# Reading the moving operand of a feed-forward kernel as two interleaved streams

## The chip, the cores and the metric

The kernel runs on one core of one Trainium2 chip. TensorE does the matrix products (its weight loads are shown as an engine of their own, PEld), VectorE (DVE), ScalarE (ACT) and GpSimd (POOL) do the rest, and SyncE (SP) issues nearly all DMAs. The metric is the device time of one execution, in microseconds; lower is better.

## The reference

A dynamic convolution over the last 7 tokens, with softmaxed weights for each token and head, is followed by a feed-forward network with a squared ReLU:

```python
# x: (8, 4096, 192), weight_gen: (8, 4096, 8, 7), w_in: (192, 2048), w_out: (2048, 192), all float32
w = exp(weight_gen - max); w = w / (sum(w) + 1e-9)
out[b, s, h] = sum over k of w[b, s, h, k] * x_padded[b, s + k, h]     # 6 zero tokens ahead of each sequence
h = out.reshape(32768, 192) @ w_in
g = relu(h) ** 2
result = g @ w_out                                                      # (32768, 192)
```

## The kernel before

**Tiling.** The 32768 tokens lie on the 128 partitions, 256 consecutive tokens (`R`) on each. A chunk is 4 such rows (`TC`) of all partitions, 512 tokens (`N`), and there are 64 chunks. For each chunk the convolution runs on VectorE with tokens on partitions. The result is then turned, so that the 192 features lie on the partitions (3 blocks of 64, `D1`, each held twice, in the lower and in the upper 64 partitions) and the 512 tokens along the free dimension. VectorE turns blocks of 32x32 (`Q` is 32) and DMAs through DRAM put the blocks in place.

**Precision.** Products are made of pairs of numbers rounded to the fast float32 format: each operand has a high and a low part (`xh`, `xl`, `gh`, `gl`; `W` and `V` hold high and low parts of the weights). ScalarE makes the high part, VectorE the low part by subtraction.

**First product, `mm1(c, j)`, matmul at L430.** Two blocks of 128 hidden features at a time: 9 terms for each, each with 64 contraction rows and 512 moving columns. The two blocks' matmuls are issued in turn, one on the lower and one on the upper 64 rows of the array, so they run side by side as a pair: 9 pairs, 18 matmuls a call. The moving operand is `xx[rows, k]`, 512 consecutive float32 of a partition.

**Activation.** `relu` (L445 to L447), `square` (L451) and `high` (L455) run on ScalarE, `low` (L459) on VectorE.

**Second product, `mm2_turned(c, fb)`, matmul at L503.** The hidden features are contracted: for each block `fb` of 128 hidden features 5 pairs of matmuls with 64 rows and 512 moving columns, the moving operand being `g[rows]`, again 512 consecutive values. Chunks 1 to 62 go this way. Chunk 0 and the last chunk use `mm2_tile` instead (L467, L476), where the activations are the stationary operand and the moving operand is a slice of `V` or of decoded weights.

**Order.** The order is written out by hand. A chunk is 8 steps `j`. In each step TensorE does `mm1(c, j)` (9 pairs) and then `mm2_turned` for the two blocks of two steps earlier (10 pairs; `LAG` is 2, the wait list is `pend`). The low parts of a step are issued on VectorE in the step after it (`late`). `sum_turned` empties the accumulators at the end of a chunk's second product. In steps 5 and 6 of the next chunk `store_turned` turns the result back in blocks of 32x32 (L522, L525), 24 small DMAs (L531) put the blocks into `o_sb` with tokens on partitions again, and one DMA (L536) writes the chunk's 4 rows of every partition to `out`. `store` (L557) does that for chunk 0 and, in three pieces, for the last chunk. All these DMAs are issued from SP's queue, as are the loads (L107, L108), the move in `sum_turned` (L514) and the turn of the convolution (L399, L404).

Of the kernel before, what the change touches and what calls it, by code (L numbers as in the profile page):

```python
# [21 lines left out]
def kernel(  # L22
# [9 lines left out]
    nc = tc.nc  # L32
# [4 lines left out]
    P = 128  # L37
    Q = 32
    HALO = K - 1
    R = B * S // P  # L40
    PPB = S // R
    TC = 4
# [26 lines left out]

    x_v = x.rearrange("b s d -> (b s) d").rearrange("(p r) d -> p r d", r=R)  # L70
    wg_v = wg.rearrange("b s h k -> (b s) (h k)").rearrange("(p r) e -> p r e", r=R)
    out_v = out.rearrange("(p r) d -> p r d", r=R)
    w_in_u = w_in.bitcast(U32)
    w_out_u = w_out.bitcast(U32).rearrange("(f p) e -> p f e", p=P)

# [8 lines left out]
    def rows_of(c):  # L84
        return (c + CPG if c < CPG else c - CPG if c < 2 * CPG else c) * TC
# [323 lines left out]
    phs, rgs, ghs, gls, accs = {}, {}, {}, {}, {}  # L409

    def mm1(c, j, ops=range(9)):
        xh, xl = xts[c]["h"], xts[c]["l"]
        if (c, 2 * j) not in phs:
            if c == 0 and j < 2:
                two = [ps_o.tile([P, N], F32, name=f"acc{b + 2 - 2 * j}") for b in range(2)]
            elif c == 0 and j % 2:
                two = [ps_o.tile([P, N], F32, name=f"acc{b}") for b in (2, 3)]
            else:
                two = [ps_h.tile([P, N], F32, name="ph") for _ in range(2)]
            phs[c, 2 * j], phs[c, 2 * j + 1] = two  # L420
        two = phs[c, 2 * j], phs[c, 2 * j + 1]
        seq = [(q, xx, k) for q, xx in ((0, xh), (0, xl), (1, xh)) for k in range(ND)]
        for n, (q, xx, k) in enumerate(seq):
            if n not in ops:
                continue
            for i in range(2):
                rows = slice(i * D1, (i + 1) * D1)
                kw = (k + i) % ND if c < N_PE else k
                w = W[rows, q, j, kw * P:(kw + 1) * P]
                nc.tensor.matmul(two[i], w, xx[rows, k], start=(n == 0), stop=(n == len(seq) - 1))  # L430

    def relu(c, fb):
        ph = phs.pop((c, fb))
# [55 lines left out]
    def mm2_turned(c, fb):  # L489
        if fb == 0:  # L490
            accs[c] = [ps_o.tile([P, N], F32, name=f"acc{t}") for t in range(4)]
        gh, gl = ghs.pop((c, fb)), gls.pop((c, fb))
        j, i = divmod(fb, 2)
        first, last = fb == 0, fb == NF - 1
        A, B = [(0, 0, gh), (0, 0, gl), (0, 1, gh)], [(2, None, gh), (2, None, gl)]
        seq = B + A if last or first else A + B
        for n, (b, q, g) in enumerate(seq):
            k = sum(1 for m in seq[:n] if m[0] == b)
            for h in range(2):
                rows = slice(h * D1, (h + 1) * D1)  # L500
                w = V[rows, fb, P:2 * P] if q is None else V[rows, fb, 2 * P * q:2 * P * q + P]
                fl = dict(start=first and k == 0, stop=last and k == (2 if b == 0 else 1))
                nc.tensor.matmul(accs[c][b + h], w, g[rows], **fl)  # L503

    works = {}

# [9 lines left out]
    def store_turned(c, part):  # L516
        X = works[c]
        if part == 0:
            o_sb = op.tile([P, TC, D], F32, name="o_sb", bufs=2)
            Y = stage.tile([P, 2, N], F32, name="raw")  # L520
            outs[c] = o_sb, Y
            nc.vector.transpose(Y[:, 0], X[:, 0])  # L522
        else:
            nc.vector.tensor_tensor(out=X[0:D1, 1], in0=X[0:D1, 1], in1=X[0:D1, 2], op=ALU.add)
            nc.vector.transpose(outs[c][1][0:D1, 1], X[0:D1, 1])  # L525
        o_sb, Y = outs[c]
        y = Y[:, part].rearrange("p (t q i) -> p q t i" if c < N_PE else "p (q t i) -> p q t i", t=TC, i=Q)
        for e in range(P // Q if part == 0 else D1 // Q):
            d0 = part * P + e * Q
            for q in range(P // Q):  # L530
                nc.sync.dma_start(  # L531
                    out=o_sb[q * Q:(q + 1) * Q, :, d0:d0 + Q],
                    in_=y[e * Q:(e + 1) * Q, q],
                )
        if part:
            nc.sync.dma_start(out=out_v[:, rows_of(c):rows_of(c) + TC, :], in_=o_sb)  # L536

    outs = {}

# [12 lines left out]
                nc.vector.tensor_tensor(out=to[:, h], in0=acc[:, h], in1=tmp[:, t, l], op=ALU.add)  # L552

    def store(c, t0, t1):
        o_sb, _ = outs[c]
        tsl = slice(t0, t1)
        nc.sync.dma_start(out=out_v[:, rows_of(c) + t0:rows_of(c) + t1, :], in_=o_sb[:, tsl])  # L557


    nc.vector.memset(warm, 0.0)  # L560
# [33 lines left out]
    for u in range(NU):  # L594
# [36 lines left out]
        if u == 0:  # L631
            for n in range(2 * ND):
                for j in range(2):
                    mm1(0, j, (n,))
            for j in range(2):
                mm1(0, j, range(2 * ND, 3 * ND))
        else:
            mm1(0, 2 * u)
            mm1(0, 2 * u + 1)
# [68 lines left out]
    for c in range(1, NCH):  # L708
        tail = c == NCH - 1
        for j in range(NJ):  # L710
# [4 lines left out]
            if c == 1 and j == 0:  # L715
                for t in range(TC // 2):
                    finish(0, t)
                store(0, 0, TC)
# [3 lines left out]
            if len(pend) == LAG or tail and pend:  # L722
                c2, j2 = pend.pop(0)
                for fb in (2 * j2, 2 * j2 + 1):
                    mm2_turned(c2, fb)
                done = c2 if j2 == NJ - 1 else None
# [15 lines left out]
            if c > 1 and j == OUT_STEP:  # L742
                store_turned(c - 1, 0)
            if c > 1 and j == OUT_STEP + 1:
                store_turned(c - 1, 1)
# [4 lines left out]
    c = NCH - 1  # L750
# [7 lines left out]
    for t in range(TC - 1):  # L758
        for fb in range(NF - 4, NF):
            mm2_tile(c, fb, t)  # L760
        finish(c, t)
        if t:
            store(c, 0 if t == 1 else t, t + 1)
    t, end = TC - 1, range(NF - 4, NF)
# [6 lines left out]
    o_sb, tmp = outs[c]  # L771
    finish(c, t, tmp[:, t, 0:D])
    nc.vector.tensor_tensor(out=o_sb[:, t], in0=rest[:, 0:D], in1=tmp[:, t, 0:D], op=ALU.add)  # L773
    store(c, t, TC)


# [28 lines left out]
```

## Time and profile before

| | |
|---|---|
| time, median of 3 runs | 2230.92 us (2230.7 to 2230.98) |
| span of the profiled execution, first to last instruction | 2229.4 us |
| TensorE busy | 2224.8 us, 19486 matmuls |
| VectorE busy | 1869.8 us |
| ScalarE busy | 1805.4 us |
| GpSimd busy | 9.9 us |
| DMA | 195.30 MB, mean 88 GB/s |

The profiled execution's own time is its span and what lies around it; the median of the runs is 1.5 us above the span. The busy time of TensorE counts overlapping matmuls once. A matmul's start is recorded; its end is modelled, so the distance between starts is the figure to read, not the duration of one.

### The profile page before, as it was taken

Reading aid. Unit: us, or ns where it says so; the run is one execution under the profiler, and the core shown is the slowest. Engines: PE = TensorE matmul, PEld = TensorE weight load, DVE = VectorE, ACT = ScalarE, POOL = GpSimd, SP = SyncE. Lnnn points to the kernel's source line nnn. Section 1 sums busy time; section 2 is a strip of 40 time slices with the busy share of each in tenths; the row PEclk is TensorE's granted clock in tenths of the full one; section 3 lists DMA queues with packets and bytes.
Section 4 is the critical chain, followed back from the end, with each engine's and each line's share of the span. In section 5 each row is a group of like instructions: output and inputs, shape, how many; then the busy total and the mean of one; then the engine's idle time right before and its main releaser. Section 6 shows DMA issues by size and latency. Waiting matters only on the chain.

```text
span 2229.4 us, 50051 instructions
## 1 busy us (share of the span) xinstructions
PE 2224.8 (100%) x19486; PEld 1846.2 (83%) x19486; DVE 1869.8 (84%) x2866; ACT 1805.4 (81%) x3492; POOL 9.9 (0%) x18
## 2 busy tenths in 40 slices
PE   9999999999999999999999999999999999999999
PEld 8888888888888888888888888888888888888888
DVE  9888888888888888888898888888888888888885
ACT  8888888888888888888888888888888888888886
POOL 0000000000000000000000000000000000000000
PEclk9999999999999999999999999999999999999999
DMA  8433323333233333333332333323333233332322
GB/s 221 96 85 92 90 59 100 83 94 99 57 92 89 88 100 75 74 95 82 100 85 64 100 85 92 88 60 100 84 94 96 54 98 86 91 100 66 82 60 53
DMA packets 323117, 195.30 MB, mean 88 GB/s; under 512 B 223944, under 2 KB 281288, under 8 KB 319040
## 3 DMA queue, kind: packets, MB, share of 16 engines
q1 hardware_dynamic: 321584, 188.58, 33.8%
q0 software_dynamic: 1296, 3.54, 0.9%
q8 instruction: 152, 2.49, 0.5%
q14 instruction: 85, 0.70, 0.1%
HBM read 106.39 MB, written 49.55 MB: 70 GB/s over the span
## 4 chain that ended last, share of the span: by engine, by line
PE 100%; POOL 0%; DVE 0%; issue 0%; POOLq 0%
PE acc L503 50%; PE ph L430 46%; PE acc L467 1%; PE acc L476 1%; PE acc L430 0%; PE acc L341 0%; PE acc L567 0%; PE ph L329 0%; PE ph L770 0%; PE acc L329 0%; PE acc L767 0%; DVE o_sb L773 0%; POOL ident masks.py:199 0%; POOL ident masks.py:197 0%; POOL ex L92 0%
## 5 line engine op out<-in xcount | busy, mean ns | idle before, releaser
L503 PE MATMUL acc<-gh,V 64*128 64x512 f32 x5952 | 1007.4, 386 | 0.0
L430 PE MATMUL ph<-xh,W 64*128 64x512 f32 x6084 | 853.9, 386 | 0.0
L447 ACT ACTIVATE rg<-ph 128x512 f32<-128x512 f32 x992 | 539.1, 597 | 351.5 <-PE ph L430 351.4
L503 PE MATMUL acc<-gl,V 64*128 64x512 f32 x3968 | 772.4, 386 | 0.0
L459 DVE TENSOR_TENSOR gl<-rg,gh 128x512 fp32r<-128x512 f32 x1008 | 644.4, 678 | 139.0 <-ACT gh L455 137.4
L430 PEld LDWEIGHTS ph<-xh,W 64*128 64x128 f32 x6084 | 569.6, 184 | 120.4 <-ACT rg L445 0.4
L503 PEld LDWEIGHTS acc<-gh,V 64*128 64x128 f32 x5952 | 557.5, 184 | 117.1
L451 ACT ACTIVATE rg<-rg 128x512 f32<-128x512 f32 x1008 | 581.3, 633 | 0.2
L455 ACT CAST gh<-rg 128x512 fp32r<-128x512 f32 x1008 | 576.1, 626 | 3.2 <-PE acc L476 3.2
L503 PEld LDWEIGHTS acc<-gl,V 64*128 64x128 f32 x3968 | 371.7, 184 | 78.0
L430 PE MATMUL ph<-xl,W 64*128 64x512 f32 x3042 | 427.3, 386 | 0.0
L266 DVE TENSOR_TENSOR pr<-xt,wt 128x768 f32<-128x768 f32 (+1 forms) x441 | 411.7, 946 | 2.3
L279 DVE TENSOR_TENSOR pr<-pr 128x768 f32<-128x768 f32 x366 | 347.0, 948 | 0.1
L430 PEld LDWEIGHTS ph<-xl,W 64*128 64x128 f32 x3042 | 284.9, 184 | 59.9
L310 DVE TENSOR_TENSOR xl<-xT,xh 128x512 fp32r<-128x512 f32 x186 | 117.7, 688 | 180.9 <-ACT xh L307 180.9
L307 ACT CAST xh<-xT 128x512 fp32r<-128x512 f32 x186 | 102.7, 624 | 0.1
L513 DVE TENSOR_TENSOR raw<-acc,raw 128x512 f32<-128x512 f32 x124 | 79.9, 686 | 5.9 <-ACT raw L511 5.9
L511 ACT COPY raw<-acc 128x512 f32<-128x512 f32 x124 | 66.6, 597 | 0.0
L237 ACT ACTIVATE wt<-wt 128x224 f32<-128x224 f32 x62 | 24.3, 392 | 47.4 <-DVE wt L236 47.4
L393 DVE STREAM_TRANSPOSE xr<-pr 128x768 f32<-128x768 f32 x62 | 60.6, 978 | 2.1
L525 DVE STREAM_TRANSPOSE raw<-raw 64x512 f32<-64x512 f32 x62 | 43.6, 704 | 2.1
L522 DVE STREAM_TRANSPOSE raw<-raw 128x512 f32<-128x512 f32 x62 | 43.7, 704 | 0.0
(93 smaller groups left out, 449.8 us busy)
## 6 DMA issues: line engine op xcount, KB each, us to landing
xT<-xd SPq DMA_DIRECT2D x124, 384.0 KB, 5.0
xt<-in_x_dram SPq DMA_DIRECT2D x30, 1344.0 KB, 6.9
out_dram<-o_sb SPq DMA_DIRECT2D x63, 384.0 KB, 2.7
xd<-xr SPq DMA_DIRECT2D x248, 96.0 KB, 2.0
o_sb<-raw SPq DMA_DIRECT2D x1488, 16.0 KB, 1.8
raw<-raw SPq DMA_DIRECT2D x62, 128.0 KB, 4.2
wt<-in_weight_gen_dram SPq DMA_DIRECT2D x31, 224.0 KB, 3.2
raw<-in_moe_w_in_dram SPq DMA_DIRECT2D x16, 192.0 KB, 5.3
```

What stands on the lines that cost most here:

```text
L266: tt(out=dst, in0=src, in1=wf[:, t0 * H:t1 * H, k:k + 1].broadcast_to([P, m, G]), op=ALU.mult)
L279: tt(out=prs[k0], in0=prs[k0], in1=prs.pop(k), op=ALU.add)
L307: nc.scalar.copy(parts["h"][:, k, n], src[k][:, n])
L310: tt(out=parts["l"][:, k, n], in0=src[k][:, n], in1=parts["h"][:, k, n].bitcast(F32), op=ALU.subtract)
L430: nc.tensor.matmul(two[i], w, xx[rows, k], start=(n == 0), stop=(n == len(seq) - 1))
L447: nc.scalar.activation(r, ph, AF.Relu)
L451: nc.scalar.activation(r, r, AF.Square)
L455: nc.scalar.copy(gh, rgs[c, fb])
L459: nc.vector.tensor_tensor(out=gl, in0=rgs.pop((c, fb)), in1=ghs[c, fb].bitcast(F32), op=ALU.subtract)
L503: nc.tensor.matmul(accs[c][b + h], w, g[rows], **fl)
L511: nc.scalar.copy(X[:, k], acc[b])
L513: nc.vector.tensor_tensor(out=X[:, k], in0=acc[b + 1], in1=X[:, k], op=ALU.add)
```

## The change

Before, both products read 512 moving columns in the order in which they lie. After it, each block of 32 columns is read as columns 0, 16, 1, 17, 2, 18 and so on, two streams 16 columns (64 bytes) apart, taken in turn. The number of columns, matmuls and weight loads stays. The output columns come out in that permuted order, so the tokens of each block of 32 are permuted once (chunk 0 and the last, where only the first product reads this way) or twice (all others). The store undoes that: instead of one DMA of 128 partitions there are four, one for each group of 32 partitions, whose DRAM side walks the partitions in the turned order (`a` is 4 for two reads and 2 for one).

```diff
-    out_v = out.rearrange("(p r) d -> p r d", r=R)
+
+    def put_out(c, t0, t1, o_sb, reads):
+        rows = slice(rows_of(c) + t0, rows_of(c) + t1)
+        v = out.rearrange("(q a b r) d -> q b a r d", q=P // Q, a=2 ** reads, r=R)
+        for q in range(P // Q):
+            nc.sync.dma_start(out=v[q, :, :, rows, :], in_=o_sb[q * Q:(q + 1) * Q, t0:t1])
+
+    def two_streams(t):
+        return t.rearrange("p (b i m) -> p b m i", i=2, m=Q // 2)
...
-                nc.tensor.matmul(two[i], w, xx[rows, k], start=(n == 0), stop=(n == len(seq) - 1))
+                nc.tensor.matmul(two[i], w, two_streams(xx[rows, k]), start=(n == 0), stop=(n == len(seq) - 1))
...
-                nc.tensor.matmul(accs[c][b + h], w, g[rows], **fl)
+                nc.tensor.matmul(accs[c][b + h], w, two_streams(g[rows]), **fl)
...
         if part:
-            nc.sync.dma_start(out=out_v[:, rows_of(c):rows_of(c) + TC, :], in_=o_sb)
+            put_out(c, 0, TC, o_sb, 2)
...
     def store(c, t0, t1):
-        o_sb, _ = outs[c]
-        tsl = slice(t0, t1)
-        nc.sync.dma_start(out=out_v[:, rows_of(c) + t0:rows_of(c) + t1, :], in_=o_sb[:, tsl])
+        put_out(c, t0, t1, outs[c][0], 1)
```

## Rows read from the trace of the kernel before

**Rows 1.** The page: busy time by engine, and the chain that ended last by line.

```profile
PE 2224.8 (100%) x19486; PEld 1846.2 (83%) x19486; DVE 1869.8 (84%) x2866; ACT 1805.4 (81%) x3492; POOL 9.9 (0%) x18
...
PE acc L503 50%; PE ph L430 46%; PE acc L467 1%; PE acc L476 1%; PE acc L430 0%; PE acc L341 0%; PE acc L567 0%; PE ph L329 0%; PE ph L770 0%; PE acc L329 0%; PE acc L767 0%; DVE o_sb L773 0%; POOL ident masks.py:199 0%; POOL ident masks.py:197 0%; POOL ex L92 0%
```

**Rows 2.** Groups by line and shape: count | busy us, mean ns | idle before us.

```profile
L503 PE MATMUL acc<-gh,V 64*128 64x512 f32 x5952 | 1007.4, 386 | 0.0
L430 PE MATMUL ph<-xh,W 64*128 64x512 f32 x6084 | 853.9, 386 | 0.0
L503 PE MATMUL acc<-gl,V 64*128 64x512 f32 x3968 | 772.4, 386 | 0.0
...
L430 PE MATMUL ph<-xl,W 64*128 64x512 f32 x3042 | 427.3, 386 | 0.0
...
L430 PE MATMUL acc<-xh,W 64*128 64x512 f32 x60 | 8.3, 391 | 0.0
...
L430 PE MATMUL acc<-xl,W 64*128 64x512 f32 x30 | 4.1, 387 | 0.0
```

**Rows 3.** Timeline of TensorE, mid-kernel: start us, us, line, operation, count.

```profile
1001.92 0.84 PE L430 MATMUL ph<-xh,W 64*128 64x512 f32 x6
1002.60 0.84 PE L430 MATMUL ph<-xl,W 64*128 64x512 f32 x6
...
1003.96 0.39 PE L503 MATMUL acc<-gh,V 64*128 64x512 f32 x2
...
1006.23 0.84 PE L430 MATMUL ph<-xh,W 64*128 64x512 f32 x6
```

**Rows 4.** Busy us of each engine in one chunk's stretch, then granted clock.

```profile
1000.00:1034.46 34.46, 34.46 (x308) 28.48 (x306) 29.14 (x45) 27.99 (x55) 0.00 (x0) 1.00 0.40 109
```

**Rows 5.** Timeline of TensorE, chunk 0's second product, plain float32.

```profile
42.74 9.26 PE L467 MATMUL acc<-du,gl 128*128 128x192 f32 x56
51.84 1.04 PE L329 MATMUL acc<-ident,wide 128*128 128x128 f32 x8
```

**Rows 6.** Waits between engines: total us, times, longest; longest and TensorE's own.

```profile
ACT rg L447 <- PE ph L430: 351.4, 371, 1.8
...
PE acc L567 <- POOL ident masks.py:199: 1.4, 1, 1.4
```

**Rows 7.** Timeline of VectorE's longest run without a gap, and the matmul that follows.

```profile
1011.12 1.90 DVE L310 TENSOR_TENSOR xl<-xT,xh 128x512 fp32r<-128x512 f32 x3 [3.01 <-ACT xh L307]
1012.94 0.95 DVE L266 TENSOR_TENSOR pr<-xt,wt 128x768 f32<-128x768 f32 x1
1013.81 0.95 DVE L279 TENSOR_TENSOR pr<-pr 128x768 f32<-128x768 f32 x1
1014.68 0.68 DVE L524 TENSOR_TENSOR raw<-raw 64x512 f32<-64x512 f32 x1
1015.39 0.70 DVE L525 STREAM_TRANSPOSE raw<-raw 64x512 f32<-64x512 f32 x1
1016.02 1.24 DVE L459 TENSOR_TENSOR gl<-rg,gh 128x512 fp32r<-128x512 f32 x2
...
1017.11 0.39 PE L503 MATMUL acc<-gl,V 64*128 64x512 f32 x2
```

**Rows 8.** Timeline of SP's queue around a chunk's store: start us, us of issue.

```profile
1025.24 0.36 SPq L536 DMA_DIRECT2D out_dram<-o_sb  x1
1025.65 0.43 SPq L107 DMA_DIRECT2D wt<-in_weight_gen_dram  x1
1026.12 0.48 SPq L108 DMA_DIRECT2D xt<-in_x_dram  x1
1026.64 0.53 SPq L514 DMA_DIRECT2D raw<-raw  x1
```

**Rows 9.** Timeline of the tail: the last stores and what releases the last one.

```profile
2224.56 2.37 SPq L557 DMA_DIRECT2D out_dram<-o_sb  x3
...
2226.21 0.36 DVE L773 TENSOR_TENSOR o_sb<-ph,raw 128x192 f32<-128x192 f32 x1
```

## The prediction

> **What bounds the kernel now.** I read the page's busy times first, then its chain of work, the groups by line, the table of waits, the timeline of TensorE in the middle, and last the timelines of VectorE, of SP's queue and of the tail. TensorE is busy for 2224.8 of 2229.4 us, and the chain that ended last is 96% the matmuls of L503 and L430 [rows 1]. None of these groups has idle time ahead of it [rows 2], and the longest wait of a matmul on another engine in the whole table is one of 1.4 us at the start; the long waits are those of ScalarE for TensorE [rows 6]. So the time is the number of matmuls times the distance between their starts, and whatever changes that distance moves the end almost one for one.
>
> The count: L503 has 5952 + 3968 = 9920 matmuls, L430 has 6084 + 3042 + 60 + 30 = 9216 [rows 2]. They run side by side in twos, so there are 9568 pairs. The distance: from the first product's start at 1001.92 to the start of the low-part pair at 1017.11 lie three steps of 19 pairs and 10 pairs more, 67 pairs in 15.19 us, 226.7 ns a pair [rows 3, 7]. All pairs together take 9568 x 0.2267 = 2169 us; the other 60 us are the start, chunk 0's second product and the tail, which the change leaves alone.
>
> The granted clock is 1.00, the 2.4 GHz level [rows 4]. At it 226.7 ns are 544 cycles, for 512 columns. That is 32 cycles more than one per column, and 544 is 512 x 17/16: as if a cycle were lost after every 16 columns, that is after every 64 bytes of float32. These 32 cycles are all that this change can win on TensorE.
>
> **Whose cycles are they?** The trace has one neighbour that helps. In chunk 0's second product 56 instructions of 192 columns take 51.84 - 42.74 = 9.10 us, 162.5 ns or 390 cycles each [rows 5]. This is plain float32, which goes in two instructions a matmul at two cycles per column: 384 cycles and 6 over. Every one of them has its own weight load, as those of a pair have. A weight load and a change of matmul thus cost some 6 cycles, not 32, where the columns are fetched at half the rate. Where they are fetched at one per cycle, 32 are lost. This points to the fetching of the moving operand, and to a loss by amount fetched; it doesn't prove it, since no row shows the fast format at another width without the weight loads being in the way.
>
> The Trainium skill has a figure for the fixed part: "TensorE: Matmul & The Clock Gate", section "Back-to-back issue gap", gives 518 cycles for 512 columns, 6 over. The 6 of the plain float32 rows agrees; the 544 of the pairs does not, and the measurement decides. By that figure a pair freed of the loss would take 215.8 ns, and the sum below would come out near 2132 us.
>
> **The change part by part.** *The order of reading.* No row shows a moving operand read in this order, so its price is bounded from both sides. Below: one column per cycle at the granted clock, 512 / 2.4 = 213.3 ns a pair, 13.3 ns less than now. Above: the slowest reading in the trace, 162.5 / 192 = 0.846 ns per column [rows 5], 433 ns a pair. In between lies no change, 226.7. I take the lower end: 544 is 512 x 17/16 to within a cycle, so the pair shows no 6 fixed cycles beside the loss (one of its two row groups is still streaming while the other changes over), and a loss that recurs each 64 bytes has a natural cure in having the next 64 bytes already open, which two streams 64 bytes apart would do: each gets a fetch only every second cycle. Gain: 9568 x 13.33 = 127.6 us.
>
> *What becomes late.* A step of 19 pairs shrinks from 4.31 to 4.05 us and a chunk from 34.46 to 32.4. VectorE's 29.14 and ScalarE's 27.99 us a chunk [rows 4] still fit, at 90% and 86%. The tightest place: VectorE starts `xl` at 1011.12, 4.89 us after the start of its step's first product at 1006.23 [rows 3, 7], and runs without a gap to the first `gl` of L459, ready about 1016.64 (half of the 1.24 us). Its consumer starts at 1017.11. The consumer comes 48 pairs after 1006.23 (two steps, nine pairs and one), 10.88 us now, 10.24 then. The producer is ready 10.41 us after 1006.23 now; its run hangs on the end of the 9 pairs of that step, so 0.12 earlier then, 10.29. The slack of 0.47 turns into a wait of 0.05 us. With 61 chunks of this kind that is 3 us; at 0.2 us each, were each operation a little late, 12; at nothing, 0. What waits behind it on TensorE is everything, so it counts whole.
>
> *The stores.* A chunk's one DMA takes 0.36 us of SP's queue [rows 8]; four take 1.44, so 1.1 us more stand ahead of the loads L107 and L108 (needed a chunk later) and of the move L514, issued at 1026.64 and used in step 6, some 20 us later. The cover is that long; without it the price would be 1.1 us a chunk, 68 in all. No wait is added and no other queue has any of it. In the tail nothing covers it: the last chunk's three stores become twelve issues. The first starts at 2224.56 [rows 9]; twelve at 0.36 fill the queue to 2228.9, where it ends at 2226.93 now (2224.56 + 2.37). Cost 1.9 us; at 0.3 us each 1.2, at 0.45 each 3.
>
> **The sum**, against the profiled execution: 2229.4 - 127.6 + 3 + 1.9 = 2106.7 us of span. The runs' median lies 1.5 us above the span, so 2108.
>
> **The rivals.**
> *1. Slower: the reading gets dearer.* If TensorE gets several neighbouring columns in one fetch and keeps no more than that, then each column of the turned order needs a fetch of its own. For this speaks that the loss shows only where columns come one per cycle, so the fetch is at its limit already. Against it speaks that the loss recurs only every 16 columns, so that at least 64 bytes must come smoothly. At the plain float32 rate a pair takes 433 ns: 2229.4 + 9568 x 0.2067 = 4207 us of span, some 4210 in all with the tail. It decides as soon as a pair costs 0.5 ns more than now, one lost cycle in 500 columns; half that size would still be 3200. The Trainium skill has a rule to this end: "SBUF — State Buffer", section "Specifications (TRN2)", says that memory lines are 16 bytes and that full bandwidth needs at least two hits on a line. In the turned order every next access is on another line. The trace neither bears it out nor refutes it, since every fast matmul in it reads in order; that its loss comes every fourth such line and not every line speaks a little against the rule being all there is.
> *2. No change: the 32 cycles aren't of the address.* They may be a fixed cost of a pair in this format, or be lost for each 16 columns delivered, in whatever order. For it: only widths of 512 run unhindered, so fixed and proportional cannot be told apart. Against it: the 6 cycles of the plain float32. Then only the tail moves: 2230.9 + 1.9 = 2233.
> *3. Half the gain.* The two streams hide one of two losses (528 cycles, 220 ns), or VectorE's wait grows to 1 us a chunk. 9568 x 6.7 ns is 64 us, giving 2172; the wait would give 2166.
>
> **How the numbers follow.** What measurement can tell from no change is about 0.2%, 4.5 us. Chances: forecast 0.54, half gain 0.08, no change 0.18 (inside the 0.2%), slower 0.20, nearly all of it far above 3000 us. So faster 0.62, same 0.18, slower 0.20. The likeliest case's own range is 2100 to 2140: from no wait at all and a short tail (2104, and a little under it) to 6 fixed cycles left in each pair. The range that holds 8 in 10 leaves out the slower rival and takes in the rest: 2098 to 2238.
>
> **What would show it.** Right: three pairs of L430 start 0.64 us apart instead of 0.68; TensorE's matmul count unchanged; a chunk of 32.4 us; waits of TensorE for `gl` of some tenths of a microsecond in step 0 of the chunks' second products; twelve issues of L557's stores at the end. Wrong by rival 1: pairs 0.43 us apart, ScalarE and VectorE idle half the time. Wrong by rival 2: 226.7 ns as before and a span 2 us longer. Wrong in size only: pairs at 213 ns but a chunk over 33 us, with TensorE waiting for ScalarE or VectorE in the table of waits.

## The result, and the profile after

The changed kernel takes 2146.36 us (median of 4 runs, 2143.92 to 2151.99) against 2230.86 us (4 runs): a ratio of 0.9625, 95% interval 0.9611 to 0.9638, 3.8% faster. The forecast was 2108 in a range of 2098 to 2238. The profiled execution is the fastest of the four, with a span of 2142.2 us; the spread of the others is wider than before; e8 below removes the wait shown here, and the spread goes with it. One of e2's four runs below took 9492.9 us, at a granted clock of 0.224; the time given for e2 is that of the other three.

The page's busy times and its chain by line, to be held against [rows 1]:

```profile
PE 2131.4 (99%) x19486; PEld 2044.4 (95%) x19486; DVE 1857.5 (87%) x2866; ACT 1797.9 (84%) x3492; POOL 9.9 (0%) x18
...
PE acc L512 49%; PE ph L439 45%; PE acc L476 1%; PE acc L485 1%; SPq L540 1%; DMA xT<-xd 0%; DVE gl L468 0%; ACT gh L464 0%; ACT rg L460 0%; DMA out_dram<-o_sb 0%; ACT rg L456 0%; DVE du L184 0%; DVE du L186 0%; PE acc L439 0%; DVE xl L319 0%
```

The count of matmuls is the same, and TensorE still carries the chain (the first product is now L439, the second L512). New in the chain are the low part of L468 and SP's queue, a little of each. The busy times of one chunk's stretch, to be held against [rows 4]:

```profile
1000.00:1032.95 32.95, 32.95 (x307) 31.77 (x306) 28.93 (x46) 27.86 (x54) 0.00 (x0) 1.00 0.31 66
```

The timeline of TensorE, to be held against [rows 3], first one undisturbed step, then the end of the next one:

```profile
1001.97 0.95 PE L439 MATMUL ph<-xh,W 64*128 64x512 f32 x6
1002.62 0.95 PE L439 MATMUL ph<-xl,W 64*128 64x512 f32 x6
...
1003.92 0.51 PE L512 MATMUL acc<-gh,V 64*128 64x512 f32 x2
...
1006.07 0.95 PE L439 MATMUL ph<-xh,W 64*128 64x512 f32 x6
...
1008.02 0.51 PE L512 MATMUL acc<-gh,V 64*128 64x512 f32 x2
1008.27 0.48 PE L512 MATMUL acc<-gl,V 64*128 64x512 f32 x2
1008.59 0.59 PE L512 MATMUL acc<-gh,V 64*128 64x512 f32 x4
```

A step of 19 pairs takes 1006.07 - 1001.97 = 4.10 us, 215.8 ns a pair instead of 226.7. The granted clock is 1.00, the 2.4 GHz level, so these are 518 cycles: 512 columns and 6. The two matmuls of a pair, which started 3 ns apart before, now start 78 and 138 ns apart by turns. At 1008.27 the rhythm breaks: the next pair comes after 0.25 and the one after it after 0.32 us instead of 0.216. The weight loads and VectorE at the same place:

```profile
1007.80 0.32 PEld L512 LDWEIGHTS acc<-gh,V 64*128 64x128 f32 x2
1008.27 0.18 PEld L512 LDWEIGHTS acc<-gl,V 64*128 64x128 f32 x2
```

```profile
1007.57 1.24 DVE L468 TENSOR_TENSOR gl<-rg,gh 128x512 fp32r<-128x512 f32 x2
```

Undisturbed, the weights of a pair are loaded while the pair before it runs, as those of 1007.80 are for the matmuls of 1008.02. Here the load for the `gl` pair starts at 1008.27 only, when the first of the two low parts (half of the 1.24 us after 1007.57) has just been written: the wait for `gl` sits on the weight load, which precedes its matmul by a whole pair. One row group alone is late by it: its matmul at 1008.27 by some 31 ns, the next one by 104 ns more. The other row group loses as much two steps later, and there it is no low part that is waited for. The load for its first matmul into an accumulator starts when VectorE has just emptied that accumulator (the addition of L522):

```profile
1016.82 0.18 PEld L512 LDWEIGHTS acc<-gh,V 64*128 64x128 f32 x1
```

```profile
1016.09 0.67 DVE L522 TENSOR_TENSOR raw<-acc,raw 128x512 f32<-128x512 f32 x1
```

So both row groups lose 0.135 us a chunk: 59 chunks take 32.94 us or more, where 152 x 0.2158 is 32.81, and a few of them lose up to 0.8 us beyond that, for a reason that is not shown here. From the first product of chunk 1 to that of chunk 63 it takes 2039.8 us, and 2030.1 in e8 below, which has none of these gaps: 9.7 us together.

SP's queue, once in mid-kernel, and in the tail with the subtraction that releases the last store, to be held against [rows 8, 9]:

```profile
983.34 3.08 SPq L77 DMA_DIRECT2D out_dram<-o_sb  x4
...
2132.67 6.98 SPq L77 DMA_DIRECT2D out_dram<-o_sb  x11
...
2133.69 0.36 DVE L780 TENSOR_TENSOR o_sb<-ph,raw 128x192 f32<-128x192 f32 x1
```

Four turned stores in mid-kernel take 3.08 us of the queue, 0.77 each, not 0.36. In the tail, where one permutation is undone and not two, eleven take 6.98 us: 0.63 each, 0.55 to 0.59 of it the issue itself. From the end of VectorE's last subtraction, at 2134.05, to the end of the span are 8.15 us; before they were 2229.4 - 2226.57 = 2.83. The tail has lost 5.3 us.

So: 2229.4 - 9568 x 0.01083 (103.6) + 9.7 + 5.3 = 2140.8, against a measured span of 2142.2. Most of the missing 1.4 us lies at the start: the first product of chunk 1 starts at 54.70 us, before the change at 54.55, so the 72 pairs of chunk 0, 0.8 us of the 103.6, gained nothing.

### The profile page after: what moved, and what is told of

Read it like the earlier page. It is cut to its first block, busy times and chain, and to the rows that moved or that the text cites. A ratio compares the mean times of both kernels' runs of the same rounds, so it can differ in the third digit from the quotient of the medians.

```text
span 2142.2 us, 50282 instructions
## 1 busy us (share of the span) xinstructions
PE 2131.4 (99%) x19486; PEld 2044.4 (95%) x19486; DVE 1857.5 (87%) x2866; ACT 1797.9 (84%) x3492; POOL 9.9 (0%) x18
## 4 chain that ended last, share of the span: by engine, by line
PE 96%; DVE 1%; SPq 1%; ACT 1%; DMA 0%; issue 0%; DVEq 0%; ACTq 0%
PE acc L512 49%; PE ph L439 45%; PE acc L476 1%; PE acc L485 1%; SPq L540 1%; DMA xT<-xd 0%; DVE gl L468 0%; ACT gh L464 0%; ACT rg L460 0%; DMA out_dram<-o_sb 0%; ACT rg L456 0%; DVE du L184 0%; DVE du L186 0%; PE acc L439 0%; DVE xl L319 0%
## 5 line engine op out<-in xcount | busy, mean ns | idle before, releaser
L512 PE MATMUL acc<-gh,V 64*128 64x512 f32 x5952 | 1085.2, 377 | 0.0
L512 PE MATMUL acc<-gl,V 64*128 64x512 f32 x3968 | 917.4, 378 | 0.6 <-DVE gl L468 0.5
L439 PE MATMUL ph<-xh,W 64*128 64x512 f32 x6084 | 917.7, 376 | 0.2
L512 PEld LDWEIGHTS acc<-gh,V 64*128 64x128 f32 x5952 | 779.9, 186 | 25.6
L468 DVE TENSOR_TENSOR gl<-rg,gh 128x512 fp32r<-128x512 f32 x1008 | 641.3, 675 | 119.6 <-ACT gh L464 119.6
L439 PEld LDWEIGHTS ph<-xh,W 64*128 64x128 f32 x6084 | 709.8, 186 | 24.8 <-issue 0.7
L512 PEld LDWEIGHTS acc<-gl,V 64*128 64x128 f32 x3968 | 556.3, 186 | 23.6 <-DVE gl L468 3.3
L439 PE MATMUL ph<-xl,W 64*128 64x512 f32 x3042 | 459.3, 376 | 0.0
L439 PEld LDWEIGHTS ph<-xl,W 64*128 64x128 f32 x3042 | 355.3, 186 | 11.6
L522 DVE TENSOR_TENSOR raw<-acc,raw 128x512 f32<-128x512 f32 x124 | 79.0, 675 | 3.8 <-ACT raw L520 3.8
```

The source lines that it names most:

```text
L439: nc.tensor.matmul(two[i], w, two_streams(xx[rows, k]), start=(n == 0), stop=(n == len(seq) - 1))
L468: nc.vector.tensor_tensor(out=gl, in0=rgs.pop((c, fb)), in1=ghs[c, fb].bitcast(F32), op=ALU.subtract)
L512: nc.tensor.matmul(accs[c][b + h], w, two_streams(g[rows]), **fl)
L522: nc.vector.tensor_tensor(out=X[:, k], in0=acc[b + 1], in1=X[:, k], op=ALU.add)
```

## The experiments

**One product at a time (e1, e2).** In the first run only L439 reads two streams, in the second only L512; the stores undo one permutation (in e2 those of chunk 0 and the last chunk undo none).

```diff
-                nc.tensor.matmul(accs[c][b + h], w, two_streams(g[rows]), **fl)
+                nc.tensor.matmul(accs[c][b + h], w, g[rows], **fl)        # e1; e2 does this to xx[rows, k]
...
-            put_out(c, 0, TC, o_sb, 2)
+            put_out(c, 0, TC, o_sb, 1)
```

> Only the first product reads two streams; the second reads in order; the store undoes one permutation by four DMAs. Theory (the loss is a property of each matmul's own moving read): pairs of the first product start 215.8 ns apart, those of the second 226.7 as before; 4608 pairs x 10.8 ns = 49.9 us gained, the tail loses 5.3, so 2230.9 - 49.9 + 5.3 = 2186, a few us more if VectorE's stall appears. Rival (the gain comes from the mix of the two products, for instance from how weight loads of one overlap reads of the other): neither product is at 215.8 and the time is not the sum of the parts: all of 2146 or nothing gained.

> Only the second product of chunks 1 to 62 reads two streams. Theory: pairs of the second product 215.8 ns apart, of the first 226.7; 4960 x 10.8 = 53.7 us gained, the tail loses 5.3: 2182, a few us more with stalls. The gains of this run and of the run with the first product only add up to that of the whole change, 103.6. Rival: not additive.

Measured: e1 2202.4 us (ratio 0.9874, 0.9860 to 0.9887), e2 2194.8 us (0.9838, 0.9823 to 0.9853). They gain 28 and 36 us, less than the 50 and 54 expected. The timeline of TensorE in e1:

```profile
1003.45 0.81 PE L439 MATMUL ph<-xh,W 64*128 64x512 f32 x6
1004.09 0.81 PE L439 MATMUL ph<-xl,W 64*128 64x512 f32 x6
...
1005.39 0.39 PE L512 MATMUL acc<-gh,V 64*128 64x512 f32 x2
...
1007.69 0.81 PE L439 MATMUL ph<-xh,W 64*128 64x512 f32 x6
```

The nine turned pairs take 1.94 us, 215.8 ns each, as expected. The ten pairs in order take 1007.69 - 1005.39 = 2.30 us, 230 ns each instead of 226.7. Pair by pair they are 229, 231, 231, 236, 228, 233 and 231 ns apart, and only the last three 226.7. So each product keeps its own rate, but reading in order is not at a fixed 226.7: this is the rhythm that it settles into after some pairs, and until then it costs more. At 0.03 us a step this is 62 x 8 x 31 ns = 15 of the 22 us by which e1 falls short of its rates; the tail is 5.3 more (its last subtraction ends 8.1 us before the end of the span, before the change 2.83). e2 falls short in the same way: its chunks take 33.81 us, where 72 pairs at 226.7 and 80 at 215.8 ns are 33.59. "Additive" is false, but not for the rival's reason.

**The stores alone (e3).** Both products in order, stores by four DMAs in plain order.

```diff
-                nc.tensor.matmul(two[i], w, two_streams(xx[rows, k]), start=(n == 0), stop=(n == len(seq) - 1))
+                nc.tensor.matmul(two[i], w, xx[rows, k], start=(n == 0), stop=(n == len(seq) - 1))
...
-                nc.tensor.matmul(accs[c][b + h], w, two_streams(g[rows]), **fl)
+                nc.tensor.matmul(accs[c][b + h], w, g[rows], **fl)
...
-            put_out(c, 0, TC, o_sb, 2)
+            put_out(c, 0, TC, o_sb, 0)
...
-        put_out(c, t0, t1, outs[c][0], 1)
+        put_out(c, t0, t1, outs[c][0], 0)
```

> Both products read in order as before; each store is four DMAs of 32 partitions in plain token order. Theory: four issues are hidden in the middle and cost only in the tail, where twelve issues of 0.6 to 0.8 us take the place of three: 5.3 us, 2236 in all; pairs at 226.7 and no wait of TensorE. The prediction's own term was 1.9 us: 2233. Rival (the stores delay loads in the queue): over 2240 with stalls of TensorE each chunk.

Measured: 2234.1 us (1.0014, 1.0005 to 1.0023), 3.3 us more. The middle is untouched (pairs at 226.7, no wait of TensorE). The instructions of the store's line, durations as minimum, median and maximum, first in e3, then in the changed kernel:

```profile
L77 SPq DMA_DIRECT2D out_dram<-o_sb x264: 314/373/1329, 54.7 to 2229.1; - x132
```

```profile
L77 SPq DMA_DIRECT2D out_dram<-o_sb x264: 554/662/1447, 55.3 to 2139.1; - x132
```

A store of the same bytes takes 0.37 us of SP's queue in plain order and 0.66 where the DRAM side walks the partitions in turned order. In e3 5.81 us lie between the last subtraction and the end of the span, 2.83 before the change and 8.15 with it. So four issues in place of one cost the tail 3.0 us and the turned order the other 2.3. Neither figure on record for this run held: 1.9 was too low for plain issues, and 5.3 needs the turned order.

**Other orders (e4, e5).** The kernel before, with the first product's order chosen by step:

```diff
+    ORDERS = [(1, 0), (2, 16), (2, 8), (2, 4), (2, 32), (2, 256), (4, 16), (-2, 16)]
+    def turned(t, j):
+        i, m = ORDERS[j]
+        if i == 1:
+            return t
+        if i < 0:
+            return t.rearrange("p (b i m) -> p i b m", i=-i, m=m)
+        return t.rearrange("p (b i m) -> p b m i", i=i, m=m)
...
-                nc.tensor.matmul(two[i], w, xx[rows, k], start=(n == 0), stop=(n == len(seq) - 1))
+                nc.tensor.matmul(two[i], w, turned(xx[rows, k], j), start=(n == 0), stop=(n == len(seq) - 1))
```

> The kernel before, but the first product's moving columns are read in another order in each of the eight steps of a chunk, so its products mix tokens and the output is not the reference's: in order; two streams 16, 8, 4, 32 and 256 columns apart; four streams 16 apart; in runs of 16 with every second run first. Read is the distance of pair starts within each step. Theory 'address' (a cycle is lost when the read leaves 64 bytes, hidden if another 64 bytes is open in turn): in order 226.7; 16, 32, 256 apart and four streams 215.8; 8 and 4 apart still lose part or all (their two streams lie in the same 64 bytes for half of the time or all of it), 220 to 227; runs of 16: 226.7. Theory 'any break of the walk' (a long in-order walk loses the cycle, whatever the distance): all turned orders 215.8, runs of 16 too. Theory 'every line change costs' (16-byte lines): 4, 8 and 16 apart all dearer than in order, already refuted for 16.

> As the run of reading orders before, with eight others in the first product: in order; two streams 2 apart; eight streams 4 apart; sixteen 2 apart; four 8 apart; thirty-two 16 apart; 128 streams 4 apart; sixteen 16 apart. The output mixes tokens. Known by now: two streams at any distance from 4 to 256 columns take 215.8 ns a pair, four streams 268.9, in order 226.7. Theory 'count' (what matters is how many streams are taken in turn, not where they lie): two streams 2 apart 215.8; four streams 8 apart 268.9 as four streams 16 apart; more streams no better than four. Theory 'two columns of a run must not follow each other' (any order that never takes neighbours is good, and the 268.9 has to do with the spacing of 16): four streams 8 apart, thirty-two 16 apart and 128 four apart at 215.8. Theory 'lines' (16-byte lines, several hits needed): thirty-two 16 apart and 128 four apart at half rate, over 400 ns.

Rows of e4's timeline, two for each of four steps; from one start to the next are three pairs. The steps are: in order, two streams 4 apart, four streams 16 apart, runs of 16.

```profile
1056.84 0.86 PE L440 MATMUL ph<-xh,W 64*128 64x512 f32 x6
1057.52 0.86 PE L440 MATMUL ph<-xl,W 64*128 64x512 f32 x6
...
1069.62 0.83 PE L440 MATMUL ph<-xh,W 64*128 64x512 f32 x6
1070.27 0.83 PE L440 MATMUL ph<-xl,W 64*128 64x512 f32 x6
...
1082.33 0.99 PE L440 MATMUL ph<-xh,W 64*128 64x512 f32 x6
1083.13 0.99 PE L440 MATMUL ph<-xl,W 64*128 64x512 f32 x6
...
1087.06 0.91 PE L440 MATMUL ph<-xh,W 64*128 64x512 f32 x6
1087.79 0.90 PE L440 MATMUL ph<-xl,W 64*128 64x512 f32 x6
```

And of e5's: two streams 2 apart, thirty-two streams 16 apart.

```profile
1373.34 0.84 PE L440 MATMUL ph<-xh,W 64*128 64x512 f32 x6
1374.02 0.84 PE L440 MATMUL ph<-xl,W 64*128 64x512 f32 x6
...
1395.35 1.46 PE L440 MATMUL ph<-xh,W 64*128 64x512 f32 x6
1396.63 1.48 PE L440 MATMUL ph<-xl,W 64*128 64x512 f32 x6
```

Mean distance of pair starts within a step, over all chunks of the trace (the first two pairs of a step left out):

| order of the moving columns | ns a pair | cycles |
|---|---|---|
| in order | 226.7 | 544 |
| two streams, 2 columns (8 bytes) apart | 226.7 | 544 |
| two streams, 4, 8, 16, 32 or 256 apart | 215.8 each | 518 |
| four streams, 8 or 16 apart | 268.9 each | 645 |
| eight streams 4 apart | 480.0 | 1152 |
| sixteen streams, 2 / 16 apart | 453 / 434 | 1088 / 1043 |
| thirty-two streams 16 apart, 128 streams 4 apart | 433, 460 | 1040, 1104 |
| runs of 16 in order, every second run first | 240.0 | 576 |

"Address" falls: 64 bytes have no part in it, since 16 bytes and 1 KB do as well. "Any break of the walk" falls with the two streams 2 apart and the runs of 16. "Count" holds for two and four streams, but for the exception of 2 apart, and more than four are no better, as it says; but it doesn't foresee that from eight on they are so much worse. "Two columns of a run must not follow each other" falls with every order of four streams or more. "Lines" foresaw the half rate of the many streams, and is contradicted by the two. Nor is it the longer access pattern as such that helps, since runs of 16 have as many dimensions as two streams. What stands is: exactly two streams, at least 16 bytes apart.

**Fewer columns (e6).**

```diff
+    WIDTHS = [(512, 0), (512, 1), (384, 0), (384, 1), (256, 0), (256, 1), (448, 0), (448, 1)]
...
-                nc.tensor.matmul(two[i], w, xx[rows, k], start=(n == 0), stop=(n == len(seq) - 1))
+                nc.tensor.matmul(two[i][:, 0:width(n, j)], w, cut(xx[rows, k], n, j), start=(n == 0), stop=(n == len(seq) - 1))
```

> The kernel before; in the first product only the first of nine terms keeps 512 columns, the other eight read fewer: by step 512 in order, 512 two streams, 384 in order, 384 two streams, 256 in order, 256 two streams, 448 in order, 448 two streams. Work is left out, so the output is not the reference's; read is the distance of pair starts. Theory 'loss by amount' (the prediction's): in order 17/16 of a cycle per column: 448 columns 476 cycles, 198.3 ns; 384 408, 170; 256 272, 113.3. Rival 'fixed loss per pair of 32 cycles': 448 200, 384 173.3, 256 120 ns. Two streams: columns + 6 cycles: 189.2, 162.5, 109.2. Rival 'weight loads': two weight loads a pair set a floor, so that 384 and 256 columns are no faster than 448, and the 215.8 ns of the two streams are this floor.

The timeline, 384 columns in order and then in two streams, three pairs from start to start:

```profile
1001.34 0.70 PE L439 MATMUL ph<-xl,W 64*128 64x384 f32 x6
1001.87 0.69 PE L439 MATMUL ph<-xh,W 64*128 64x384 f32 x6
...
1005.24 0.80 PE L439 MATMUL ph<-xl,W 64*128 64x384 f32 x6
1005.72 0.80 PE L439 MATMUL ph<-xh,W 64*128 64x384 f32 x6
```

Means: two streams 189.2, 162.5 and 111.3 ns at 448, 384 and 256 columns, that is the columns and 6 cycles (at 256, 11). In order 203.3, 178.1 and 119.0, that is 40, 43 and 30 cycles over, and not at all steady; the commonest value at 256 columns is 120 ns, 288 cycles, 32 over. "Loss by amount" asked for 28, 24 and 16 and is refuted. A loss per matmul of some 30 to 43 cycles, whatever its width, fits. The weight loads set no floor at 215.8, since pairs go down to 111 ns.

**Who collides with whom (e7, e9, e10).** e7 gives the two row groups different orders and the weights a step; e9 turns the issue round and leaves one row group out; e10 loads fewer stationary columns.

```diff
+    MIXES = [("o", "o", 1), ("s", "o", 1), ("o", "s", 1), ("o", "o", 2), ("o", "o", 4), ("s", "s", 4), ("o", "o", 16), ("e", "e", 1)]
...
-                w = W[rows, q, j, kw * P:(kw + 1) * P]
-                nc.tensor.matmul(two[i], w, xx[rows, k], start=(n == 0), stop=(n == len(seq) - 1))
+                nc.tensor.matmul(two[i], stepped(rows, q, kw, j), way(xx[rows, k], MIXES[j][i]), start=(n == 0), stop=(n == len(seq) - 1))
```

> The kernel before; the first product by step: in order; two streams on the lower row group only; on the upper only; in order with weights read with a step of 2; of 4 columns; two streams with weights in steps of 4; in order with weights in steps of 16; even columns first, then odd ones. Other weights than the reference's are taken, the output is not its. Theory 'the moving read alone': the step of the weights changes nothing, 226.7 in order and 215.8 in two streams; one row group in two streams leaves 226.7, set by the other. Rival 'collision of the moving read with the weight loads': the step of the weights moves the in-order pairs, towards 215.8 or above 227. Rival 'collision of the two row groups' reads with each other': two streams on one side alone is enough, 215.8, whichever side it is.

```diff
+    SIDES = [((0, 1), (0,)), ((1, 0), (0,)), ((1, 0), (1,)), ((1, 0), ()), ((0,), ()), ((0,), (0,)), ((1,), ()), ((1,), (1,))]
...
-            for i in range(2):
+            for i in SIDES[j][0] if n else (0, 1):
...
+                if i in SIDES[j][1]:
+                    m = m.rearrange("p (b i m) -> p b m i", i=2, m=16)
...
```

> The kernel before; in the first product, terms 2 to 9 by step: lower row group issued first and alone in two streams (known: 215.8 ns a pair); upper issued first, lower in two streams; upper first, upper in two streams; upper first, both in order; lower row group only, in order; lower only, two streams; upper only, in order; upper only, two streams (the last four leave half of the work out, so the output is not the reference's). Theory 'the one issued first pays': with the upper first, two streams on the upper give 215.8 and on the lower 226. Rival 'the lower rows pay': two streams on the lower give 215.8 in whatever order of issue. If the loss needs two row groups at once, one group alone in order takes 215.8 ns a matmul; if a weight load and an in-order read are enough, 226 or so.

```diff
+    LOADS = [(128, False), (112, False), (96, False), (80, False), (66, False), (128, True), (96, True), (66, True)]
...
+                cols, turned = LOADS[j] if n else (P, False)
+                w = W[rows, q, j, kw * P:kw * P + cols]
...
```

> The kernel before; in the first product, terms 2 to 9 load fewer stationary columns, by step: 128, 112, 96, 80 and 66 in order, then 128, 96 and 66 in two streams (outputs left out, so not the reference's). Theory 'collision with the weight loads': the loss of in-order pairs shrinks with the load, 32 cycles at 128, about 28, 24, 20 and 16 or less: 225, 223.3, 221.7, 220 ns, if the 6 cycles of the change-over are not hidden a little less gain; two streams stay at 215.8. Rival 'a fixed loss per matmul in order': 226.7 at every size.

e9's timeline, first the lower row group alone in order, then alone in two streams; no matmul of the upper group starts in either stretch, and three matmuls lie between the starts:

```profile
1001.33 0.84 PE L436 MATMUL ph<-xl,W 64*128 64x512 f32 x3
1002.01 0.39 PE L436 MATMUL ph<-xh,W 64*128 64x512 f32 x1
...
1005.60 0.81 PE L436 MATMUL ph<-xl,W 64*128 64x512 f32 x3
1006.25 0.38 PE L436 MATMUL ph<-xh,W 64*128 64x512 f32 x1
```

One row group alone shows the same 0.68 and 0.65 us: the loss needs no second row group. (The upper alone takes 215.8 ns turned and 224 to 236 in order.) With both at work, in e7 with one side turned, the turned side's matmuls start 215.8 ns apart and the other's 226.7, whichever side it is, and the two drift apart. So a group in order pays, lower or upper, issued first or second; neither "the first issued" nor "the lower rows" names who does. A turned group does not always keep its rate, though. Of e9's three steps with one side turned, two show 215.8 ns for that side (with the lower turned and issued first its last distance is 225); where the upper was issued first, in order, and the lower turned, the lower ran ahead of the other, had one distance of 320 ns and then went on at 226.7. That is the figure which "the one issued first pays" asked for. Why the turned group is held there no run shows.

Two steps of e7: two streams with weights at a step of 4, and even columns first:

```profile
1140.17 0.88 PE L444 MATMUL ph<-xl,W 64*128 64x512 f32 x6
1140.87 0.88 PE L444 MATMUL ph<-xh,W 64*128 64x512 f32 x6
...
1149.60 1.55 PE L444 MATMUL ph<-xl,W 64*128 64x512 f32 x6
1150.96 1.55 PE L444 MATMUL ph<-xh,W 64*128 64x512 f32 x6
```

Weights read with a step cost both orders: in order 231.1, 234.7 and 235.0 ns at steps of 2, 4 and 16, two streams 233.6 at a step of 4. So the weight loads bear on the distance, as the rival of collision has it. But with fewer stationary columns the in-order loss doesn't shrink: 226.7, 228.9, 229.6, 233.6 and 226.7 ns at 128, 112, 96, 80 and 66 columns, with two streams at 215.8, 215.6 and 215.8. The shrinking loss that e10's theory asked for is refuted; its rival, 226.7 at every size, holds at two sizes of five.

**The wait (e8) and the tail (e11).** e8 is the changed kernel with `OUT_STEP` 4 instead of 5. e11 is e8 with the last chunk read in order and stored as before:

```diff
-    OUT_STEP = 5
+    OUT_STEP = 4
...
-                nc.tensor.matmul(two[i], w, two_streams(xx[rows, k]), start=(n == 0), stop=(n == len(seq) - 1))
+                nc.tensor.matmul(two[i], w, xx[rows, k] if c == NCH - 1 else two_streams(xx[rows, k]), start=(n == 0), stop=(n == len(seq) - 1))
...
-        put_out(c, t0, t1, outs[c][0], 1)
+        if c < NCH - 1:
+            put_out(c, t0, t1, outs[c][0], 1)
+        else:
+            out_v = out.rearrange("(p r) d -> p r d", r=R)
+            nc.sync.dma_start(out=out_v[:, rows_of(c) + t0:rows_of(c) + t1, :], in_=outs[c][0][:, t0:t1])
```

> The changed kernel with the turned store moved from steps 5 and 6 to steps 4 and 5. Theory (each chunk loses 0.135 us, of which 0.104 is a wait for the first low part after the subtraction of L319, late because the turn and the addition of the store, L533 and L534, 1.4 us, stand ahead of it on VectorE): the wait goes, about 8 of the 10.5 us come back, 2138. Rival (the wait moves to the next step or to the SP queue): no change, 2146, with waits elsewhere.

> The changed kernel with the turned store one step earlier (2134.2 measured) and, in the last chunk alone, the first product in order and each of its three stores one DMA again. Theory (the tail loses 5.3 us to twelve issues of 0.55 to 0.77 us): these come back, and 72 pairs go back to 227 to 231 ns, 0.8 to 1.1 us: 2134.2 - 5.3 + 1.0 = 2129.9. The prediction's own figure for the tail, 1.9 us, would give 2133.3. Rival: the tail's length is set by landing, not issue: 2135.

e8: 2134.16 us (0.9566, 0.9550 to 0.9582), 12 us better than the change by the medians and 9.8 by the profiled spans (2132.4 against 2142.2), more than the 8 expected. In its table of waits the weight loads hardly wait for the low part any more; ahead of it stands the same row of the changed kernel:

```profile
PEld acc L512 <- DVE gl L468: 3.3, 9, 0.9
```

```profile
PEld acc L512 <- DVE gl L468: 0.6, 2, 0.4
```

The 104 ns gaps are gone from both row groups, and so are the longer losses: chunks 2 to 62 take 32.81 us each (152 x 0.2158), and the runs' spread is back to 1.3 us. e11: 2129.05 us (0.9542, 0.9529 to 0.9555), 5.1 better again. SP's queue in its tail:

```profile
2118.86 3.06 SPq L77 DMA_DIRECT2D out_dram<-o_sb  x4
2122.70 2.37 SPq L568 DMA_DIRECT2D out_dram<-o_sb  x3
```

The last three stores end after 2.37 us as in [rows 9]. This version beats both kernels.

## Why the prediction was right, and where its sizes were off

*The bound* held: the gain is the count of pairs times the change in their distance, 103.6 us gross, of which the waits, the tail and the start leave 87.2 us of span.

*The direction* held for a reason that did not. I took the 32 cycles for a loss by amount, one cycle each 64 bytes, because 544 is 512 x 17/16. e6 refutes that and fits a loss per matmul, whatever its width, and e4 shows that 64 bytes mean nothing. The 17/16 was a coincidence, and the sign of the result owes something to luck: by the same reasoning four streams 16 apart should have won as much, and they take 268.9 ns. That the moving read is where the cycles go, the other half of the argument, stands: e4 turned nothing else and got them back.

*The lower end for a pair*, 213.3 ns, was the first mis-sized term. From the same coincidence I concluded that a pair hides its 6 fixed cycles, one row group streaming while the other changes over. It does not: before the change both groups changed over within 3 ns of each other, and with the change they start 78 to 138 ns apart and the 6 cycles are still there. The pair measured 215.8 ns, so 103.6 us and not 127.6. "TensorE: Matmul & The Clock Gate" of the Trainium skill, section "Back-to-back issue gap", with its 518 cycles, agrees with the turned pairs to the cycle; the sum that went with it, 2132, came nearer than mine. For reads in order the trace keeps contradicting it.

*The wait* stood at the right place and was the second mis-sized term: 3 us predicted, 9.7 measured, inside the bound of 12. At 215.8 ns the low part is ready just in time for its matmul (48 x 0.2158 = 10.36 us after the step's start, ready after 10.32). But it is the weight load that waits for it, and that wants to start a pair earlier. That the other row group would wait for an accumulator (L522) was not foreseen. e8 moved the store's work on VectorE away, and both waits are gone.

*The tail* was the third: 1.9 predicted, 5.3 measured, above the bound of 3. I priced a turned store by the plain one of [rows 8], 0.36 us; in the tail one takes 0.55 to 0.59, 0.63 from start to start. Even in plain order the twelve cost 3.0 us (e3), at 0.31 to 0.43 each. The cover of the stores in the middle held (e3, and e8 with turned stores: no chunk is longer for them).

*The rivals.* No change is out. Half the gain is out in its form, though the net gain of 84.5 us lies between it and the forecast. The dearer reading is out for two streams, but real: with eight streams or more a pair takes 433 to 480 ns, the very price that the rival gave. The rule of the Trainium skill's page "SBUF — State Buffer", section "Specifications (TRN2)", that a 16-byte line needs two hits for full bandwidth, is not borne out as I applied it: two streams change the line at every column and are the fastest order of all, while even columns first has two hits in a row on each line and takes 452.6 ns a pair (e7). Only the orders of many streams behave as it says.

*What stays open* is why reading in order loses some 32 cycles a matmul and two streams do not. The runs leave a meeting of the moving read with the weight loads as the likeliest place: a step in the weights makes both orders slower, one row group alone shows the loss, and the in-order distance wanders between 224 and 236 ns before it settles. But the loss doesn't follow the size of the load, and no run was free of weight loads, so this is argued and not shown.

## What to carry to other kernels

Where a kernel is a dense train of fast-float32 matmuls, compare the distance of their starts with one cycle per column, and try the moving operand as two interleaved streams at least 16 bytes apart before anything else is moved; four streams or strided columns are worse than in order. (Here that was tried with 64 rows, mostly 512 columns, and a weight load for each matmul.) When TensorE gets faster, look for the operand that is ready last against the start of its weight load, not of its matmul. Price a store by its own access pattern, above all the last one, which nothing covers.

## What the runs showed of the hardware that was not expected

- Two interleaved streams are the only order found that reads float32 at one column per cycle and 6 cycles over: 518 cycles for 512 columns, at distances of 4, 8, 16, 32 and 256 columns. In order it is 544, four streams 645, eight or more 1040 to 1152.
- The in-order loss has a state: after a stretch of turned pairs, in-order ones take up to 236 ns and settle at 226.7 after about seven pairs, so that in e1 and e2 a mixture of the two orders gained 28 and 36 us where the rates alone promise 50 and 54.
- The two row groups can run at their own rates: with one turned and one in order their matmuls start 215.8 and 226.7 ns apart at the same time (e7), and a wait delays one group and not the other. In one step of e9 the turned group was held to 226.7.
- A DMA of 32 partitions takes a median of 0.37 us of SP's queue to issue in plain order (e3), 0.55 to 0.59 with one permutation undone (the changed kernel's tail) and a median of 0.66 over all stores of the changed kernel.
